# Two bf16 matrices packed into 4-byte words for the TensorE transposes of a sliding-window attention backward pass

## The chip, the cores and the metric

The kernel runs on one core of a Trainium2 chip. The core has five engines that work side by side and wait for each other through semaphores: TensorE (PE; the loading of its stationary operand is shown apart, as PEld), VectorE (DVE), ScalarE (ACT), GpSimd (POOL) and SyncE (SP), which here only issues DMAs. Matmuls write to PSUM; the other operands lie in SBUF. The metric is the device time of one execution in microseconds (us), the median of several runs.

## The reference

One forward pass and all of its gradients. The forward pass mixes a sliding-window attention branch and a gated feed-forward branch, with S = 2048 rows, D = 512, 32 heads of 16, a window of 256 and F = 1376, all in bf16:

```python
def _A_ref(x, wqkv, wo):
    H = 32; Dh = D // H; W = 256
    q, k, v = ...
    scores = einsum("bhqd,bhkd->bhqk", q, k) * (Dh ** -0.5)
    mask = (idx[:, None] - idx[None, :] >= 0) & (idx[:, None] - idx[None, :] < W)
    p = softmax(where(mask, scores, -1e9), axis=-1)
    o = einsum("bhqk,bhkd->bhqd", p, v)
    return merge_heads(o) @ wo

def _B_ref(x, W_gate, W_up, W_down):
    gate = x @ W_gate; up = x @ W_up
    gate = gate * (gate > 0)
    return (gate * up) @ W_down

g = sigmoid((x * gate_w).sum(-1))
out = g * _A_ref(x, ...) + (1 - g) * _B_ref(B_x, ...)
```

The kernel returns `out` and the gradients of x, wqkv, wo, W_gate, W_up, W_down and gate_w for a given grad_out.

## The kernel before

It has three phases, one after the other in time. The first (up to about 260 us of the span) is the feed-forward branch, forward and backward. The third (from about 790 us) computes the output and the gradient of x, row block by row block. The second, between them, is the attention branch, forward and backward in one sweep, and the change lies in it.

**Units.** The attention phase works through 360 units, listed in `units`. A unit is a group `c` of 8 heads (there are four), a block `j` of 128 queries, a block `kb` of 128 keys and a `half`: the four even or the four odd heads of the group (`HH` = 4). A query block sees three key blocks: its own (role "d", diagonal), the one before (role "m", middle) and the one before that (role "f", far). For a full query block the order is middle, far, diagonal for one half and middle, diagonal, far for the other.

**What one unit does.** `front` (L643 on) issues the scores matmul ST (L649, keys by 4 heads x 128 queries, 512 columns) and ACT's exponential of it, Pu (L655); for diagonal and far units POOL then clears the masked part (L657, L660). `front_dp` issues the matmul dPT (L669), the gradient with respect to the probabilities. `gradp` multiplies Pu by dPT on DVE into Pd (L674). `rowsum` issues eight small matmuls, for each of the four heads one with Pu as the stationary operand (L683) and one with Pd (L685), which add into BA. `flip` (L694 on) transposes Pu and Pd, so that queries lie on the partitions: for most diagonal units by one DMA transpose (L697), for the others by eight TensorE transposes (L706, four of Pu and four of Pd, each 128 x 128 with the identity `ident` as the moving operand) into one PSUM tile `pt` of 128 x 1024 bf16, which ACT and DVE copy to SBUF (`p2`) in turns, through the helper `evac` (L72 ACT, L74 DVE). `cd_piece` uses the transposed halves as stationary operands of eight small matmuls per unit (L488, L491), which add into CD, the gradients of keys and values; ACT copies CD out (L494).

**Order.** It is written out by hand in the main loop, one unit per iteration `n`. An iteration issues, in this order: `front` of unit n, `gradp` of unit n-1, the DMA transpose of unit n-2 if it has one, `rowsum` and the TensorE `flip` of unit n-3, `front_dp` of unit n, one or two `cd_piece`s from a queue, and, by a running credit, pieces of background work (the projections of the next heads and rows, L129 and L132, and weight gradients, L588 and L591). Each engine takes its instructions in that order.

**Buffers.** Middle and far units keep Pu and Pd in tiles of their own, with four buffers each; diagonal units keep both halves side by side in one tile `PP`, four buffers. The transposed tiles `p2` have six buffers for diagonal units, five for middle and four for far ones. `pt` has two PSUM buffers, CD and BA one each, and ST, dPT and the projections share four.

Of the kernel before, what the change touches and what calls it, by code (L numbers as in the profile page):

```python
# [8 lines left out]
ACT = mybir.ActivationFunctionType  # L9
ALU = mybir.AluOpType  # L10
AX = mybir.AxisListType
BF = mybir.dt.bfloat16
F32 = mybir.dt.float32
# [9 lines left out]
def kernel(  # L23
# [20 lines left out]
    nc = tc.nc  # L44
    P = 128
# [7 lines left out]
    Dh = D // H  # L53
# [13 lines left out]
    def evac(out, in_, eng=None):  # L67
        if eng is None:
            eng = ("act", "dve")[rr["i"] % 2]
            rr["i"] += 1  # L70
        if eng == "act":
            nc.scalar.copy(out, in_)  # L72
        elif eng == "dve":
            nc.vector.tensor_copy(out, in_)  # L74
        else:
            nc.gpsimd.tensor_copy(out, in_)
# [10 lines left out]

    cpool = ctx.enter_context(tc.tile_pool(name="const", bufs=1))
    ident = cpool.tile([P, P], BF, name="ident")
    gw_b = cpool.tile([P, D], BF, name="gw_b")  # L90
    g_all = cpool.tile([P, NT], F32, name="g_all")
    omg_all = cpool.tile([P, NT], F32, name="omg_all")
# [20 lines left out]
    if True:  # L113
        HH = HG // 2
# [74 lines left out]
    with ExitStack() as p1, tc.manual_schedule():  # L189
# [39 lines left out]
        nc.vector.memset(tiny[:], 0.0)  # L229
        nc.scalar.activation(tiny[:], tiny[:], ACT.Sigmoid)  # L230
        make_identity(nc, ident[:])
        wps0 = ps1.tile([P, TGW], F32, tag="mm", bufs=3, name="warm_ps")
        for _ in range(WARM):
            nc.tensor.matmul(wps0[:], lhsT=warm[:, 0:P], rhs=warm[:], start=True, stop=True)
# [76 lines left out]
        for fc in range(FC):  # L311
            for tg in range(NTG):
                k = Step()
# [90 lines left out]
        for n in range(N1 + 8):  # L404
# [22 lines left out]
            if at(6):  # L427
                f = weights(at(6))
# [30 lines left out]
    if True:  # L459
# [4 lines left out]
        wk = p3b.enter_context(tc.tile_pool(name="attw", bufs=2))  # L464
        pps = ExitStack()
        ps = pps.enter_context(tc.tile_pool(name="attps", bufs=2, space=PSUM))
# [6 lines left out]
        P2 = {}  # L473
# [6 lines left out]
        def cd_piece(c, kb, qb, half, last):  # L480
            if (c, kb) not in CDs:
                CDs[(c, kb)] = [ps.tile([P, HG, 2 * Dh], F32, tag="CD", bufs=1, name="CD"), True]
            cd = CDs[(c, kb)]
            rq = RQ[(c, qb)]
            p2 = P2[(c, qb, kb, half)]
            for hh in range(HH):
                h = 2 * hh + half
                nc.tensor.matmul(cd[0][:, h, :], lhsT=p2[:, 0, hh, :], rhs=rq[:, h, 0:2 * Dh],  # L488
                                 start=cd[1], stop=True, skip_group_check=True)
                cd[1] = False  # L490
                nc.tensor.matmul(cd[0][:, h, 0:Dh], lhsT=p2[:, 1, hh, :], rhs=rq[:, h, 2 * Dh:3 * Dh],  # L491
                                 start=False, stop=True, skip_group_check=True)
            if last:
                nc.scalar.copy(sts[c][:, kb, 1:3, :].rearrange("p a (h d) -> p h a d", h=HG),  # L494
                               cd[0][:].rearrange("p h (a d) -> p h a d", a=2))
                if kb == NT // 2 - 1 or (kb == NT - 1 and c == DC - 1):
                    spill(c, kb + 1 - NT // 2)

        def spill(c, t0):
            tsl = slice(t0, t0 + NT // 2)  # L500
            eng = nc.gpsimd if (c == DC - 1 and t0 > 0) else nc.sync
            eng.dma_start(dqkvo_d[t0 * P:(t0 + NT // 2) * P, c * 4 * P:(c + 1) * 4 * P].rearrange("(t p) n -> p t n", p=P),
                          sts[c][:, tsl, :, :].rearrange("p t a n -> p t (a n)"))
# [124 lines left out]
        for c in range(DC):  # L628
            for j in range(NT):
                kbs = [k for k in (j - 1, j, j - 2) if k >= 0]  # L630
                for half in range(2):
                    order = kbs if half or len(kbs) < 3 else [kbs[0], kbs[2], kbs[1]]
                    for ki, kb in enumerate(order):
                        u = Unit()
# [8 lines left out]
        def front(u):  # L643
            tg, jl = u.j // TPG, u.j % TPG
            z = zt[(u.c * NTG + tg) % ZB]
            KTt = proj[(u.c, u.kb // TPG)][f"K{u.half}"]
            ksl = slice((u.kb % TPG) * P, (u.kb % TPG + 1) * P)
            ST = ps.tile([P, HH, P], F32, tag="M", bufs=4, name="ST")
            nc.tensor.matmul(ST[:], lhsT=KTt[:, ksl], rhs=z[:, 0, jl, :, :], start=True, stop=True)  # L649
            if u.role == "d":  # L650
                u.PP = wk.tile([P, 2, HH, P], BF, tag="PP", bufs=4, name="PP")
                u.Pu, u.Pd = u.PP[:, 0, :, :], u.PP[:, 1, :, :]
            else:
                u.Pu = wk.tile([P, HH, P], BF, tag="Pu", bufs=4, name="Pu")
            nc.scalar.activation(u.Pu[:], ST[:], ACT.Exp)  # L655
            if u.role == "d":
                nc.gpsimd.affine_select(out=u.Pu[:], in_=u.Pu[:], compare_op=ALU.is_ge, fill=0.0, base=0,  # L657
                                        pattern=[[0, HH], [1, P]], channel_multiplier=-1)
            elif u.role == "f":
                nc.gpsimd.affine_select(out=u.Pu[:], in_=u.Pu[:], compare_op=ALU.is_ge, fill=0.0, base=-1,  # L660
                                        pattern=[[0, HH], [-1, P]], channel_multiplier=1)

        def front_dp(u):
# [5 lines left out]
            nc.tensor.matmul(u.dPT[:], lhsT=VTt[:, ksl], rhs=z[:, 1, jl, :, :], start=True, stop=True)  # L669

        def gradp(u):
            if u.role != "d":
                u.Pd = wk.tile([P, HH, P], BF, tag="Pd", bufs=4, name="Pd")
            nc.vector.tensor_tensor(out=u.Pd[:], in0=u.Pu[:], in1=u.dPT[:], op=ALU.mult)  # L674

        def rowsum(u):
            kv = proj[(u.c, u.kb // TPG)]["kv"]
# [16 lines left out]
        def flip(u):  # L694
            if u.dma:
                p2 = wk.tile([P, 2, HH, P], BF, tag="P2d", bufs=6, name="p2")
                nc.sync.dma_start_transpose(out=p2[:].rearrange("p a h q -> p (a h) q"),  # L697
                                            in_=u.PP[:].rearrange("p a h q -> p (a h q)"))
                P2[(u.c, u.j, u.kb, u.half)] = p2
                return  # L700
            eng = ("act", "dve")[copier["i"] % 2]
            copier["i"] += 1
            pt = ps.tile([P, 2, HH, P], BF, tag="TR", name="pt")
            for a, src in enumerate((u.Pu, u.Pd)):
                for hh in range(HH):
                    nc.tensor.transpose(pt[:, a, hh, :], src[:, hh, :], ident[:])  # L706
            p2 = wk.tile([P, 2, HH, P], BF, tag=f"P2{u.role}", bufs={"d": 6, "m": 5, "f": 4}[u.role], name="p2")
            evac(p2[:], pt[:], eng)
            P2[(u.c, u.j, u.kb, u.half)] = p2

        def small_ops(c, j, s):
            rows = proj[(c, j // TPG)]["rows"]
# [87 lines left out]
        with tc.manual_schedule():  # L800
# [20 lines left out]
            while n <= NU + LAG or ev or cdq or bgq:  # L821
                now = ev.pop(n, [])
                u = units[n] if n < NU else None
# [22 lines left out]
                if 1 <= n <= NU:  # L846
                    gradp(units[n - 1])
# [3 lines left out]
                if 2 <= n < NU + 2 and units[n - 2].dma:  # L851
                    flip(units[n - 2])
                if LAG <= n < NU + LAG:
                    w = units[n - LAG]
# [18 lines left out]
                for _ in range(2 if len(cdq) > 6 or (len(cdq) > 1 and cdq[1][5] and cdq[1][0] <= n and cdq[1][2] < NT - 1) else 1):  # L873
                    if cdq and cdq[0][0] <= n:
                        cd_piece(*cdq.pop(0)[1:])
                        credit -= 0.2
# [43 lines left out]
    with ExitStack() as p56:  # L920
        x_r5 = x_r

        with ExitStack() as p6:
# [5 lines left out]
            for g in range(NG):  # L929
# [3 lines left out]
                for tl in range(GT):  # L933
# [8 lines left out]
                    for c in range(DC):  # L942
# [16 lines left out]
                                            op=ALU.mult)  # L959
# [62 lines left out]
```

## Time and profile before

| | |
|---|---|
| median of three runs | 984.72 us (984.12 to 984.91) |
| the profiled execution's span | 983.5 us |
| PE busy | 949.9 us, 97%, 11528 matmuls |
| PEld busy | 612.1 us, 62% |
| DVE / ACT / POOL busy | 507.4 / 487.5 / 486.4 us |
| mean granted TensorE clock | 0.993 of full speed |
| TensorE transposes at L706 | 1888, of which 32 for diagonal units |
| BA matmuls, L683 and L685, of middle and far units | 928 and 928 |
| CD matmuls, L488 and L491, of all units | 1440 and 1440 |

A row of a group names line, engine, operation, what is written and read, the tile's shape (partitions x elements) and the count; then its busy time in us, the mean ns of one, and the idle time of the engine just ahead of it with what ended that. In matmul rows the moving operand is named first and the stationary one second, so `pt<-ident,Pd` streams the identity past a stationary Pd. Matmuls are pipelined: the record of one lasts until its last result has come out, so the rate is read from the distance between two starts and not from the length of a record. A line of the busy times by stretch gives the stretch in us, its length, then for PE, PEld, DVE, ACT and POOL the busy time and the number of instructions, and at last the granted clock, the DMA engines' share and GB/s.

### The profile page before, as it was taken

The page shows a single profiled execution, that of the slowest core. Times are in us where ns is not written, and L with a number is a line of the kernel's source. Part 1 is how long each engine was busy: PE and PEld are TensorE (multiplying, and loading weights), DVE is VectorE, ACT ScalarE, POOL GpSimd, SP SyncE. Part 2 cuts the span into 40 slices and gives each one's busy share as a digit, 9 for nine tenths or more (in the row PEclk, how much of TensorE's full clock was granted, in tenths as well). Part 3 has the DMA queues.
Part 4 walks back from the last instruction along what each step waited for, and adds up shares of the span by engine and source line. Part 5 has one row for each costly group of instructions (what it writes and reads, how often), then busy time and mean ns, then how long its engine had stood idle before and what let it go on. Part 6 is the DMA issues. An engine that isn't in the chain of part 4 may idle for free.

```text
span 983.5 us, 28082 instructions
## 1 busy us (share of the span) xinstructions
PE 949.9 (97%) x11528; PEld 612.1 (62%) x11528; DVE 507.4 (52%) x934; ACT 487.5 (50%) x825; POOL 486.4 (49%) x935
## 2 busy tenths in 40 slices
PE   8999999999999999999999999999999999999993
PEld 5555555666567777677676777766777744444441
DVE  4443322233477777666676666766666513223221
ACT  5422222222378877677686777767777611001000
POOL 1644345444176667655676566665656612221220
PEclk9999999999999999999999999999999999999997
DMA  9989999997546777765759556799969887788720
GB/s 283 195 186 214 214 214 225 213 200 172 134 82 100 98 137 134 137 119 92 132 103 175 119 86 133 109 151 155 167 108 212 178 225 195 199 202 202 175 56 16
DMA packets 415201, 153.55 MB, mean 156 GB/s; under 512 B 333568, under 2 KB 412768, under 8 KB 415072
## 3 DMA queue, kind: packets, MB, share of 16 engines
q1 hardware_dynamic: 392672, 128.67, 67.6%
q10 hardware_dynamic: 20592, 17.84, 6.3%
q0 software_dynamic: 1808, 5.24, 1.5%
q8 instruction: 90, 1.47, 0.6%
q14 instruction: 39, 0.32, 0.1%
HBM read 38.44 MB, written 38.41 MB: 78 GB/s over the span
## 4 chain that ended last, share of the span: by engine, by line
PE 83%; DMA 5%; issue 3%; POOL 3%; DVE 2%; ACT 1%; SPq 1%; ACTq 0%; POOLq 0%; DVEq 0%
PE pt L706 10%; PE ST L649 8%; PE dPT L669 7%; PE dxps L968 7%; PE wps L373 6%; PE BA L683 5%; PE pp L129 4%; PE wps L588 4%; PE dxps L985 4%; PE CD L488 4%; PE bps L939 4%; PE dhps L326 3%; PE dps L375 3%; PE ups L326 3%; PE gps L326 2%
## 5 line engine op out<-in xcount | busy, mean ns | idle before, releaser
L674 DVE TENSOR_TENSOR Pd<-Pu,dPT 128x512 bf16<-128x512 bf16 x232 | 154.5, 677 | 68.3 <-POOL Pu L660 59.1
L655 ACT ACTIVATE Pu<-ST 128x512 bf16<-128x512 f32 x232 | 139.0, 601 | 62.6 <-PE ST L649 60.1
L649 PE MATMUL ST<-z,K 128*128 128x512 bf16 x360 | 136.0, 378 | 3.9 <-DVE wst_end L74 1.2
L669 PE MATMUL dPT<-z,V 128*128 128x512 bf16 x360 | 136.1, 378 | 0.5
L72 ACT COPY p<-pt 128x1024 bf16<-128x1024 bf16 x118 | 119.6, 1014 | 12.2 <-PE pt L706 9.3
L657 POOL TENSOR_SCALAR_AFFINE_SELECT PP<-PP 128x512 bf16<-128x512 bf16 x128 | 81.2, 634 | 79.0 <-ACT PP L655 77.9
L340 POOL TENSOR_TENSOR hT<-rg,upm 128x512 bf16<-128x512 bf16 x44 | 52.3, 1189 | 124.7 <-DVE upm L338 97.1
L488 PE MATMUL CD<-rq,p 128*128 128x32 bf16 x1440 | 109.4, 177 | 1.6 <-ACT rows_st L494 1.6
L373 PE MATMUL wps<-dgu_r,x_r 128*128 128x256 bf16 x704 | 105.6, 273 | 4.8 <-DVE wst L74 4.8
L491 PEld LDWEIGHTS <-p 128*128 128x128 bf16 x1440 | 86.1, 96 | 35.5 <-issue 1.9
L491 PE MATMUL CD<-rq,p 128*128 128x16 bf16 x1440 | 106.6, 169 | 0.0
L488 PEld LDWEIGHTS <-p 128*128 128x128 bf16 x1440 | 98.8, 96 | 1.0 <-issue 0.7
L674 DVE TENSOR_TENSOR PP<-PP,dPT 128x512 bf16<-128x512 bf16 x128 | 87.3, 682 | 23.1 <-POOL PP L657 20.9
L373 PEld LDWEIGHTS <-x_r 128*128 128x128 bf16 x704 | 68.8, 98 | 36.5 <-issue 6.1
L706 PE MATMUL pt<-ident,Pd 128*128 128x128 bf16 x928 | 89.7, 219 | 0.0
L655 ACT ACTIVATE PP<-ST 128x512 bf16<-128x512 f32 x128 | 77.1, 602 | 25.0 <-PE ST L649 22.5
L706 PE MATMUL pt<-ident,Pu 128*128 128x128 bf16 x928 | 89.0, 217 | 0.0
L74 DVE COPY p<-pt 128x1024 bf16<-128x1024 bf16 x118 | 81.1, 687 | 14.3 <-PE pt L706 13.1
L660 POOL TENSOR_SCALAR_AFFINE_SELECT Pu<-Pu 128x512 bf16<-128x512 bf16 x112 | 71.0, 634 | 32.6 <-ACT Pu L655 32.0
L946 ACT COPY a_sb<-aps 128x512 f32<-128x512 f32 x16 | 9.4, 585 | 145.8 <-issue 133.1
L685 PEld LDWEIGHTS <-Pd 128*128 128x128 bf16 x928 | 57.6, 96 | 35.0 <-issue 12.2
L683 PE MATMUL BA<-KV,Pu 128*128 128x33 bf16 x928 | 76.7, 178 | 1.8 <-ACT BAs L689 1.4
(154 smaller groups left out, 1969.5 us busy)
## 6 DMA issues: line engine op xcount, KB each, us to landing
dqkvo_d<-rows_st SPq DMA_DIRECT2D x7, 1024.0 KB, 5.8
dar<-da_d SPq DMA_DIRECT2D x28, 256.0 KB, 4.6
hT_d<-hT ACTq DMA_DIRECT2D x44, 128.0 KB, 2.6
dgT_d<-dgu ACTq DMA_DIRECT2D x44, 128.0 KB, 3.0
duT_d<-dgu ACTq DMA_DIRECT2D x44, 128.0 KB, 2.9
duT_g<-duT_d SPq DMA_DIRECT2D x8, 640.0 KB, 5.3
dgT_g<-dgT_d SPq DMA_DIRECT2D x7, 640.0 KB, 5.1
gt<-hT_d SPq DMA_DIRECT2D x7, 640.0 KB, 5.6
```

The source lines that it names most:

```text
L72: nc.scalar.copy(out, in_)
L74: nc.vector.tensor_copy(out, in_)
L373: nc.tensor.matmul(acc["w"][:, c, :], lhsT=x_r[:, t, c * P:(c + 1) * P], rhs=k.dgu_r[:, :, i, :], start=(go_ and c % 2 == 0), stop=no_, sk ...
L488: nc.tensor.matmul(cd[0][:, h, :], lhsT=p2[:, 0, hh, :], rhs=rq[:, h, 0:2 * Dh], start=cd[1], stop=True, skip_group_check=True)
L491: nc.tensor.matmul(cd[0][:, h, 0:Dh], lhsT=p2[:, 1, hh, :], rhs=rq[:, h, 2 * Dh:3 * Dh], start=False, stop=True, skip_group_check=True)
L649: nc.tensor.matmul(ST[:], lhsT=KTt[:, ksl], rhs=z[:, 0, jl, :, :], start=True, stop=True)
L655: nc.scalar.activation(u.Pu[:], ST[:], ACT.Exp)
L657: nc.gpsimd.affine_select(out=u.Pu[:], in_=u.Pu[:], compare_op=ALU.is_ge, fill=0.0, base=0, pattern=[[0, HH], [1, P]], channel_multiplier=-1)
L669: nc.tensor.matmul(u.dPT[:], lhsT=VTt[:, ksl], rhs=z[:, 1, jl, :, :], start=True, stop=True)
L674: nc.vector.tensor_tensor(out=u.Pd[:], in0=u.Pu[:], in1=u.dPT[:], op=ALU.mult)
L683: nc.tensor.matmul(BA[:, h, 0:33], lhsT=u.Pu[:, hh, :], rhs=kv[:, u.kb % TPG, h, 1:34], start=(u.first and hh == 0), stop=True, skip_group ...
L706: nc.tensor.transpose(pt[:, a, hh, :], src[:, hh, :], ident[:])
```

## The change

For middle and far units, Pu and Pd no longer have tiles of their own. One tile W of 128 x 4 x 128 fp32 words is allocated in `front`. Seen as bf16, each word is a pair: Pd is the lower half of every word and Pu the upper half. The exponential, POOL's select and DVE's product write and read their half with a step of two bf16 (4 bytes), and so do the BA matmuls that take Pu and Pd as the stationary operand. `flip` transposes W as fp32, with an fp32 identity `ident_w` made at the start: four transposes of 128 x 128 words per unit in place of eight of 128 x 128 bf16. The PSUM tile has the same bytes (512 fp32 in place of 1024 bf16 per partition), and ACT and DVE copy it out as fp32 in the same turns. `cd_piece` then takes the two halves of the copied words, again with a step of two bf16. Diagonal units keep their layout and their transposes. The number of buffers for W is four.

```diff
@@ -87,6 +87,7 @@
 
     cpool = ctx.enter_context(tc.tile_pool(name="const", bufs=1))
     ident = cpool.tile([P, P], BF, name="ident")
+    ident_w = cpool.tile([P, P], F32, name="ident_w")
     gw_b = cpool.tile([P, D], BF, name="gw_b")
     g_all = cpool.tile([P, NT], F32, name="g_all")
     omg_all = cpool.tile([P, NT], F32, name="omg_all")
@@ -229,6 +230,7 @@
         nc.vector.memset(tiny[:], 0.0)
         nc.scalar.activation(tiny[:], tiny[:], ACT.Sigmoid)
         make_identity(nc, ident[:])
+        make_identity(nc, ident_w[:])
         wps0 = ps1.tile([P, TGW], F32, tag="mm", bufs=3, name="warm_ps")
         for _ in range(WARM):
             nc.tensor.matmul(wps0[:], lhsT=warm[:, 0:P], rhs=warm[:], start=True, stop=True)
@@ -485,10 +487,10 @@
             p2 = P2[(c, qb, kb, half)]
             for hh in range(HH):
                 h = 2 * hh + half
-                nc.tensor.matmul(cd[0][:, h, :], lhsT=p2[:, 0, hh, :], rhs=rq[:, h, 0:2 * Dh],
+                nc.tensor.matmul(cd[0][:, h, :], lhsT=p2[0][:, hh, :], rhs=rq[:, h, 0:2 * Dh],
                                  start=cd[1], stop=True, skip_group_check=True)
                 cd[1] = False
-                nc.tensor.matmul(cd[0][:, h, 0:Dh], lhsT=p2[:, 1, hh, :], rhs=rq[:, h, 2 * Dh:3 * Dh],
+                nc.tensor.matmul(cd[0][:, h, 0:Dh], lhsT=p2[1][:, hh, :], rhs=rq[:, h, 2 * Dh:3 * Dh],
                                  start=False, stop=True, skip_group_check=True)
             if last:
                 nc.scalar.copy(sts[c][:, kb, 1:3, :].rearrange("p a (h d) -> p h a d", h=HG),
@@ -651,13 +653,15 @@
                 u.PP = wk.tile([P, 2, HH, P], BF, tag="PP", bufs=4, name="PP")
                 u.Pu, u.Pd = u.PP[:, 0, :, :], u.PP[:, 1, :, :]
             else:
-                u.Pu = wk.tile([P, HH, P], BF, tag="Pu", bufs=4, name="Pu")
-            nc.scalar.activation(u.Pu[:], ST[:], ACT.Exp)
+                u.W = wk.tile([P, HH, P], F32, tag="W", bufs=4, name="W")
+                pair = u.W[:].bitcast(BF).rearrange("p h (q w) -> p h q w", w=2)
+                u.Pd, u.Pu = pair[:, :, :, 0], pair[:, :, :, 1]
+            nc.scalar.activation(u.Pu, ST[:], ACT.Exp)
             if u.role == "d":
-                nc.gpsimd.affine_select(out=u.Pu[:], in_=u.Pu[:], compare_op=ALU.is_ge, fill=0.0, base=0,
+                nc.gpsimd.affine_select(out=u.Pu, in_=u.Pu, compare_op=ALU.is_ge, fill=0.0, base=0,
                                         pattern=[[0, HH], [1, P]], channel_multiplier=-1)
             elif u.role == "f":
-                nc.gpsimd.affine_select(out=u.Pu[:], in_=u.Pu[:], compare_op=ALU.is_ge, fill=0.0, base=-1,
+                nc.gpsimd.affine_select(out=u.Pu, in_=u.Pu, compare_op=ALU.is_ge, fill=0.0, base=-1,
                                         pattern=[[0, HH], [-1, P]], channel_multiplier=1)
 
         def front_dp(u):
@@ -669,9 +673,7 @@
             nc.tensor.matmul(u.dPT[:], lhsT=VTt[:, ksl], rhs=z[:, 1, jl, :, :], start=True, stop=True)
 
         def gradp(u):
-            if u.role != "d":
-                u.Pd = wk.tile([P, HH, P], BF, tag="Pd", bufs=4, name="Pd")
-            nc.vector.tensor_tensor(out=u.Pd[:], in0=u.Pu[:], in1=u.dPT[:], op=ALU.mult)
+            nc.vector.tensor_tensor(out=u.Pd, in0=u.Pu, in1=u.dPT[:], op=ALU.mult)
 
         def rowsum(u):
             kv = proj[(u.c, u.kb // TPG)]["kv"]
@@ -696,17 +698,26 @@
                 p2 = wk.tile([P, 2, HH, P], BF, tag="P2d", bufs=6, name="p2")
                 nc.sync.dma_start_transpose(out=p2[:].rearrange("p a h q -> p (a h) q"),
                                             in_=u.PP[:].rearrange("p a h q -> p (a h q)"))
-                P2[(u.c, u.j, u.kb, u.half)] = p2
+                P2[(u.c, u.j, u.kb, u.half)] = (p2[:, 0, :, :], p2[:, 1, :, :])
                 return
             eng = ("act", "dve")[copier["i"] % 2]
             copier["i"] += 1
-            pt = ps.tile([P, 2, HH, P], BF, tag="TR", name="pt")
-            for a, src in enumerate((u.Pu, u.Pd)):
-                for hh in range(HH):
-                    nc.tensor.transpose(pt[:, a, hh, :], src[:, hh, :], ident[:])
-            p2 = wk.tile([P, 2, HH, P], BF, tag=f"P2{u.role}", bufs={"d": 6, "m": 5, "f": 4}[u.role], name="p2")
+            if u.role == "d":
+                pt = ps.tile([P, 2, HH, P], BF, tag="TR", name="pt")
+                for a, src in enumerate((u.Pu, u.Pd)):
+                    for hh in range(HH):
+                        nc.tensor.transpose(pt[:, a, hh, :], src[:, hh, :], ident[:])
+                p2 = wk.tile([P, 2, HH, P], BF, tag="P2d", bufs=6, name="p2")
+                evac(p2[:], pt[:], eng)
+                P2[(u.c, u.j, u.kb, u.half)] = (p2[:, 0, :, :], p2[:, 1, :, :])
+                return
+            pt = ps.tile([P, HH, P], F32, tag="TR", name="pt")
+            for hh in range(HH):
+                nc.tensor.transpose(pt[:, hh, :], u.W[:, hh, :], ident_w[:])
+            p2 = wk.tile([P, HH, P], F32, tag=f"P2{u.role}", bufs={"m": 5, "f": 4}[u.role], name="p2")
             evac(p2[:], pt[:], eng)
-            P2[(u.c, u.j, u.kb, u.half)] = p2
+            pair = p2[:].bitcast(BF).rearrange("p h (k w) -> p h k w", w=2)
+            P2[(u.c, u.j, u.kb, u.half)] = (pair[:, :, :, 1], pair[:, :, :, 0])
 
         def small_ops(c, j, s):
             rows = proj[(c, j // TPG)]["rows"]
```

## The prediction

> **What bounds the kernel now.** I read the page first, then the busy times by stretches of the span, the chain of waits inside the attention loop, the timeline of one iteration, and the groups of instructions by shape.
>
> ```profile
> PE 949.9 (97%) x11528; PEld 612.1 (62%) x11528; DVE 507.4 (52%) x934; ACT 487.5 (50%) x825; POOL 486.4 (49%) x935
> ...
> PE 83%; DMA 5%; issue 3%; POOL 3%; DVE 2%; ACT 1%; SPq 1%; ACTq 0%; POOLq 0%; DVEq 0%
> ...
> 267.00:780.00 513.00, 507.20 (x8834) 369.77 (x8833) 361.21 (x657) 381.35 (x641) 332.88 (x775) 1.00 0.73 130
> ```
>
> PE has 83% of the chain that ended last. The third line is the stretch that the change touches, the attention loop (first transpose at 267.2 us, last at 779.4): 513 us, PE busy for 507, DVE 361, ACT 381, POOL 333, granted clock 1.00. Before it lie 267 us (feed-forward) and after it 204 us (output phase), which hold none of the edited work.
>
> Busy PE time is modelled, so I go by the distance from one start to the next, which the timeline gives:
>
> ```profile
> 501.02 0.17 PE L685 MATMUL BA<-KV,Pd 128*128 128x17 bf16 x1
> 501.04 0.18 PE L683 MATMUL BA<-KV,Pu 128*128 128x33 bf16 x1
> 501.07 0.17 PE L685 MATMUL BA<-KV,Pd 128*128 128x17 bf16 x1
> 501.09 0.18 PE L683 MATMUL BA<-KV,Pu 128*128 128x33 bf16 x1
> ...
> 501.19 0.38 PE L706 MATMUL pt<-ident,Pu 128*128 128x128 bf16 x4
> 501.41 0.39 PE L706 MATMUL pt<-ident,Pd 128*128 128x128 bf16 x4
> 501.64 0.38 PE L669 MATMUL dPT<-z,V 128*128 128x512 bf16 x1
> 501.85 0.18 PE L488 MATMUL CD<-rq,p 128*128 128x32 bf16 x1
> ```
>
> Small matmuls, each with its own weight load, follow each other every 25 ns. Eight transposes take from 501.19 to 501.64, 0.45 us, 56 ns each. A matmul of 512 columns holds PE for 0.215 us (501.64 to 501.85). Taking every PE matmul of the loop at such a distance gives 497 us; the remaining 15 us are longer gaps, most of them between ST and the first BA matmul. So PE's in-order stream is the loop's clock, and a nanosecond added to or taken from that stream shows up nearly in full, until another engine's chain takes over.
>
> ```profile
> L706 PE MATMUL pt<-ident,Pd 128*128 128x128 bf16 x928 | 89.7, 219 | 0.0
> L706 PE MATMUL pt<-ident,Pu 128*128 128x128 bf16 x928 | 89.0, 217 | 0.0
> L685 PEld LDWEIGHTS <-Pd 128*128 128x128 bf16 x928 | 57.6, 96 | 35.0 <-issue 12.2
> L683 PE MATMUL BA<-KV,Pu 128*128 128x33 bf16 x928 | 76.7, 178 | 1.8 <-ACT BAs L689 1.4
> L72 ACT COPY p<-pt 128x1024 bf16<-128x1024 bf16 x118 | 119.6, 1014 | 12.2 <-PE pt L706 9.3
> L74 DVE COPY p<-pt 128x1024 bf16<-128x1024 bf16 x118 | 81.1, 687 | 14.3 <-PE pt L706 13.1
> ```
>
> 928 + 928 transposes over 8 make 232 changed units (the other 32 at this line belong to four diagonal units, which stay). They hold PE for 232 x 0.45 = 104.4 us.
>
> **The change, part by part.**
>
> *Transposes.* 1856 of 128 bf16 columns become 928 whose data and identity are fp32. No row has a 4-byte operand on PE, so the price is bounded. From below: a column costs the same whatever its width, 56 ns, and the unit goes from 0.45 to 0.224 us, -52.4 us over 232 units. From above: a word is two 16-bit halves in the data and two in the identity, so four products of 128 columns, which is a 512-column row, 0.215 us, 0.86 us per unit, 199.5 us in all, **+95.1 us**. Break-even is 112 ns. I take the upper end: all rows from 128 to 512 columns cost strictly by column of 2-byte numbers, and nothing in the trace shows the array taking more than 2 bytes per operand in a step; a transpose that has to return all 32 bits unchanged can drop none of the products.
>
> The Trainium skill, "FP8 and Floating Point Precision", TensorE Precision Notes, says that true fp32 takes four passes through the array; by it the sum would be 928 x 4 x 56 = 208 us, +103.5 us. No run so far shows an fp32 matmul here.
>
> *Weight loads.* Pu and Pd, and their transposed halves, are now every second bf16 of a row. They are the weights of 8 BA and 8 CD matmuls per unit, 16 x 232 = 3712 loads. From below they cost nothing more: 25 ns is also the distance of 17-column and 33-column matmuls alike, so something other than the operand sets it. From above, the overlap is lost and the whole 96 ns of a load's record shows: 71 ns x 3712 = +264 us. I take 0, being nearest to the same instruction with the same 128 columns, and keep the upper end as a rival.
>
> *Exp, select and product* write and read at a 4-byte step: 232 exp (601 ns), 112 selects (634 ns), 232 products (677 ns). The products already have a 4-byte operand, dPT in PSUM. Even 100 ns more on each puts ACT at 381 + 23 and DVE at 361 + 23 of 513 us, so other iterations' PE work hides it: 0. Were PE no longer the cover, the chain exp, select, product would be 0.3 us longer per far unit, 112 x 0.3 = 34 us at most.
>
> *Copies out of PSUM.* ACT's 118 copies go from 1024 bf16 (1014 ns) to 512 fp32; the nearest row, a_sb of 512 fp32 from PSUM, takes 585 ns, so ACT loses 118 x 0.43 = 51 us of work. DVE's go from 687 to about the 692 ns of its 512-element fp32 casts. Neither is on the path: no PE wait in the loop names these copies. Worth 0, at best a part of the 15 us of gaps.
>
> *Buffers and the rest.* W holds Pu and Pd from the exp on, four buffers as each had before. Units run middle, far, diagonal, middle, diagonal, far, so the fifth changed unit is six iterations after the first, whose transposes come three iterations after its exp: no new wait. The second identity adds a memset and a select on POOL (0.20 and 0.29 us for the first) ahead of a 12.4 us idle stretch; with no such cover it would be 0.5 us. No DMA is added or moved, on any queue.
>
> *The gaps.* Slower transposes give the exp, select, product chain 0.41 us more per unit, which covers part of the 15 us; I take half, -8 us (bounds 0 and -15).
>
> Sum against the profiled execution: span 983.5 + 95.1 - 8 = 1070.6 us. The median of the runs is 984.7, 1.2 us more than that span, so **1072 us**. This case's own range, with the gaps from 0 to -15 and the transpose at 54 to 56 ns a pass, is 1064 to 1090.
>
> **Rivals.**
>
> *One pass, priced by bytes.* 128 words are as many bytes as 256 columns of bf16, and the 256-column rows of the feed-forward phase are 108 ns apart. The unit then takes 0.434 us: -0.016 x 232 = -3.7 us, **981 us**, with 0 to -15 for gaps that the lighter ACT closes and some tens of nanoseconds per unit the other way, 966 to 992. For it: all PE rows scale with bytes as well as with columns. Against: it needs the array to carry 32 bits through in one go.
>
> *One pass at the column rate* (the other side). PE reads a word as easily as a half and returns it whole: 56 ns, -52.4 us, 932 us; the iteration gets shorter, and up to 15 us comes back as waits of PE for the exp, select, product chain, which already make the gaps. **940 us**, 932 to 950. It decides from a transpose under 112 ns. For it: cost by column is the only rule that the rows state. Against: all of them are bf16.
>
> The Trainium skill, "TensorE: Matmul & The Clock Gate", Terms, lists a transpose mode that is 4x faster for fp32; by that rule this rival holds. No row here shows it.
>
> *The load is exposed.* If the weight load of a 4-byte tile isn't overlapped with the transpose before it, each costs 96 + 56 = 152 ns, 0.61 us a unit, +0.16 x 232 = 37 us, **1021 us**. Against: every load in the rows above is hidden.
>
> The same page of the skill, Weight-path perf modes, leaves fp32 out of its fast weight load.
>
> *Strided weights.* If half of each word read is thrown away and a pair goes from 25 to 50 ns, 3712 x 25 = +93 us on top of any of these; with the one pass by bytes **1074 us**, with the forecast 1165. Its limit is the +264 us above. Against: the 25 ns doesn't look like the load's own time.
>
> **How the numbers follow.** Forecast 0.38; one pass by bytes 0.25; one pass by column 0.12; exposed load 0.12; strided weights 0.13. A measurement of this kernel (984.1 to 984.9) can tell about 0.2%, 2 us. The one-pass-by-bytes case straddles zero: of its 0.25 I give 0.14 to faster, 0.06 to same, 0.05 to slower. Faster is 0.12 + 0.14 = 0.26, same 0.06, slower 0.38 + 0.12 + 0.13 + 0.05 = 0.68. The range takes in all but the upper part of the strided case: from 932 (the column rate without any loss) to 1100.
>
> **What would show it.** In the changed profile, the line of the fp32 transposes: their number (928 if a word goes through in one instruction, more if it is split), and the distance from the first transpose of a unit to the dPT matmul after it: 0.86 us by the forecast, 0.43, 0.22 and 0.61 by the rivals. BA and CD pairs must stay 25 ns apart; if they are wider, strided weights are at work. ACT's copies should be near 585 ns, and the stretch before 267 us unchanged. A transpose under 112 ns with 25 ns pairs makes the prediction wrong.

## The result and the profile after

The changed kernel takes 992.88 us (median of four runs, 992.63 to 994.99) beside 984.42 us for the kernel before (four runs): a ratio of 1.0090, 95% interval 1.0076 to 1.0104. The profiled execution's span is 991.3 us, against 983.5 before. The change is slower, as forecast, but by 8.5 us and not by 87.

The page of the changed kernel, its busy times, its chain and the groups that answer to those of before (line, engine, operation, shapes and count; then busy us and mean ns of one; then idle time before):

```profile
PE 955.6 (96%) x10600; PEld 615.1 (62%) x10600; DVE 515.3 (52%) x934; ACT 479.5 (48%) x825; POOL 499.2 (50%) x937
...
PE 76%; POOL 9%; DVE 4%; issue 4%; DMA 4%; ACT 1%; SPq 1%; ACTq 0%; POOLq 0%; DVEq 0%
...
L659 ACT ACTIVATE W<-ST 128x512 bf16<-128x512 f32 x232 | 175.6, 758 | 80.8 <-PE ST L651 74.2
L676 DVE TENSOR_TENSOR W<-W,dPT 128x512 bf16<-128x512 bf16 x232 | 166.7, 734 | 79.9 <-POOL W L664 72.7
L716 PE MATMUL pt<-ident_w,W 128*128 128x128 f32 x928 | 147.4, 281 | 0.0
...
L664 POOL TENSOR_SCALAR_AFFINE_SELECT W<-W 128x512 bf16<-128x512 bf16 x112 | 85.8, 766 | 33.3 <-ACT W L659 31.6
...
L716 PEld LDWEIGHTS pt<-ident_w,W 128*128 128x128 f32 x928 | 97.2, 141 | 0.0
L659 ACT ACTIVATE PP<-ST 128x512 bf16<-128x512 f32 x128 | 76.8, 600 | 31.6 <-PE ST L651 27.4
```

The same three operations of the kernel before:

```profile
L674 DVE TENSOR_TENSOR Pd<-Pu,dPT 128x512 bf16<-128x512 bf16 x232 | 154.5, 677 | 68.3 <-POOL Pu L660 59.1 <-PE dPT L669 6.9 <-PE ST L649 1.3
L655 ACT ACTIVATE Pu<-ST 128x512 bf16<-128x512 f32 x232 | 139.0, 601 | 62.6 <-PE ST L649 60.1
...
L660 POOL TENSOR_SCALAR_AFFINE_SELECT Pu<-Pu 128x512 bf16<-128x512 bf16 x112 | 71.0, 634 | 32.6 <-ACT Pu L655 32.0
```

Three things are to be seen. There are 928 fp32 transposes, one instruction per four-byte tile, so nothing was split into passes that show. The strided exp (758 ns against 601 before, and 600 for the diagonal units, which still write at unit step), select (766 against 634 before) and product (734 against 677) are all longer; exp and select by more than the 100 ns that I allowed for. And POOL and DVE have 13% of the chain that ended last, where they had 5%.

The timeline of one unit of the changed kernel:

```profile
502.28 0.18 PE L685 MATMUL BA<-KV,W 128*128 128x33 bf16 x1
502.31 0.17 PE L687 MATMUL BA<-KV,W 128*128 128x17 bf16 x1
502.33 0.63 PE L716 MATMUL pt<-ident_w,W 128*128 128x128 f32 x4
502.81 0.38 PE L673 MATMUL dPT<-z,V 128*128 128x512 bf16 x1
```

BA pairs are still 25 ns apart, although their weights are strided. The four transposes hold PE from 502.33 to 502.81. From the single starts in the trace, the first takes 144 ns until the next starts and the other three 109 ns each: 471 ns a unit, where eight bf16 transposes took 444. (The start of the first is the usual 25 ns behind the last BA matmul; the extra 35 ns lie between its start and that of the second.)

For all runs I use one ledger, worked out from the starts of the PE matmuls: the loop is the time from the first ST to the last CD; the transposes are the usual time per unit times the number of units (with 1.8 us for the four diagonal ones); all other matmuls at their usual distance are 408.7 us in every kernel; what remains are gaps. Each row is one profiled execution. What lies outside the loop stayed between 450.0 and 453.5 us in all executions of this table and of the one further down, and the loop's difference to the kernel before agrees with that of the medians to within 2.8 us, so a difference of gaps below 2 or 3 us says little by itself. In four traces (marked *) some of the 512-column records are missing, so the gaps there are this remainder, and what is counted from single gaps is approximate.

| kernel | loop, us | transposes, us (ns a unit) | gaps, us | ratio to before (95%) |
|---|---|---|---|---|
| before | 530.9 | 104.7 (444) | 17.5 | 1 |
| changed | 539.1 | 111.1 (471) | 19.3 | 1.0090 (1.0076 to 1.0104) |
| layout alone* | 536.3 | 104.7 (444) | 22.9 | 1.0058 (1.0042 to 1.0075) |
| fp32 transposes alone* | 535.4 | 111.1 (471) | 15.6 | 1.0056 (1.0040 to 1.0071) |
| changed, word exp | 535.7 | 111.1 (471) | 15.9 | 1.0058 (1.0038 to 1.0077) |
| changed, dPT first* | 534.9 | 102.6 (434) | 23.6 | 1.0049 (1.0033 to 1.0065) |
| before, dPT first* | 533.2 | 104.9 (444) | 19.6 | 1.0046 (1.0028 to 1.0064) |
| changed, transposes first | 534.6 | 102.9 (436) | 23.0 | 1.0040 (1.0026 to 1.0054) |
| before, transposes first | 527.2 | 105.0 (445) | 13.4 | 0.9960 (0.9946 to 0.9974) |
| before, copies as words | 531.1 | 104.7 (444) | 17.6 | 1.0008 (0.9996 to 1.0020) |

Between the two kernels the loop grew by 8.2 us: 6.4 in the transposes and 1.8 in the gaps. The 1.8 is small beside the spread, but the waits counted below grow by as much.

### The profile page after: what moved, and what is told of

It is laid out like the page before. It is cut to its first block, busy times and chain, and to the rows that moved or that the text cites. A ratio compares the mean times of both kernels' runs of the same rounds, so it can differ in the third digit from the quotient of the medians.

```text
span 991.3 us, 26230 instructions
## 1 busy us (share of the span) xinstructions
PE 955.6 (96%) x10600; PEld 615.1 (62%) x10600; DVE 515.3 (52%) x934; ACT 479.5 (48%) x825; POOL 499.2 (50%) x937
## 4 chain that ended last, share of the span: by engine, by line
PE 76%; POOL 9%; DVE 4%; issue 4%; DMA 4%; ACT 1%; SPq 1%; ACTq 0%; POOLq 0%; DVEq 0%
PE pt L716 8%; PE dxps L979 7%; PE wps L375 6%; PE ST L651 6%; PE dPT L673 6%; PE pp L130 4%; PE wps L590 4%; PE dxps L996 4%; PE bps L950 4%; PE BA L685 3%; PE CD L490 3%; PE dhps L328 3%; PE dps L377 3%; PE ups L328 3%; PE gps L328 3%
## 5 line engine op out<-in xcount | busy, mean ns | idle before, releaser
L659 ACT ACTIVATE W<-ST 128x512 bf16<-128x512 f32 x232 | 175.6, 758 | 80.8 <-PE ST L651 74.2
L676 DVE TENSOR_TENSOR W<-W,dPT 128x512 bf16<-128x512 bf16 x232 | 166.7, 734 | 79.9 <-POOL W L664 72.7
L716 PE MATMUL pt<-ident_w,W 128*128 128x128 f32 x928 | 147.4, 281 | 0.0
L664 POOL TENSOR_SCALAR_AFFINE_SELECT W<-W 128x512 bf16<-128x512 bf16 x112 | 85.8, 766 | 33.3 <-ACT W L659 31.6
L716 PEld LDWEIGHTS pt<-ident_w,W 128*128 128x128 f32 x928 | 97.2, 141 | 0.0
L74 DVE COPY p<-pt 128x512 f32<-128x512 f32 x118 | 80.7, 684 | 10.8 <-PE pt L716 10.6
L687 PEld LDWEIGHTS <-W 128*128 128x128 bf16 x928 | 57.9, 97 | 33.6 <-issue 10.9
L685 PEld LDWEIGHTS <-W 128*128 128x128 bf16 x928 | 68.3, 97 | 15.9 <-issue 2.5
L685 PE MATMUL BA<-KV,W 128*128 128x33 bf16 x928 | 76.7, 178 | 1.5 <-ACT BAs L691 1.5
```

The lines of the kernel that those rows point to most:

```text
L659: nc.scalar.activation(u.Pu, ST[:], ACT.Exp)
L664: nc.gpsimd.affine_select(out=u.Pu, in_=u.Pu, compare_op=ALU.is_ge, fill=0.0, base=-1, pattern=[[0, HH], [-1, P]], channel_multiplier=1)
L676: nc.vector.tensor_tensor(out=u.Pd, in0=u.Pu, in1=u.dPT[:], op=ALU.mult)
L685: nc.tensor.matmul(BA[:, h, 0:33], lhsT=u.Pu[:, hh, :], rhs=kv[:, u.kb % TPG, h, 1:34], start=(u.first and hh == 0), stop=True, skip_group ...
L716: nc.tensor.transpose(pt[:, hh, :], u.W[:, hh, :], ident_w[:])
```

## Experiments

**The two halves of the change, each alone.** My theory after the result: PE's own time for the transposes makes the whole loss. Rival: the slower exp, select and product make it.

```diff
-            pt = ps.tile([P, HH, P], F32, tag="TR", name="pt")
-            for hh in range(HH):
-                nc.tensor.transpose(pt[:, hh, :], u.W[:, hh, :], ident_w[:])
...
+            pt = ps.tile([P, 2, HH, P], BF, tag="TR", name="pt")
+            for a, src in enumerate((u.Pu, u.Pd)):
+                for hh in range(HH):
+                    nc.tensor.transpose(pt[:, a, hh, :], src[:, hh, :], ident[:])
...
```

> The interleaved tile W alone: exp, select and product write and read every second bf16, BA takes its weights from them, but each unit is transposed as before by eight bf16 transposes (from strided weights), copied out as 1024 bf16, and CD's weights are contiguous. Theory (the loss is PE's: the four fp32 transposes of a unit take 479 ns where eight bf16 ones took 444): the loss is gone, 984 to 986 us, ratio to before 1.000 to 1.002, a unit's transposes again 444 ns, although exp stays near 758 ns, select near 766 and product near 734. Rival (the slower exp, select and product delay PE): about as slow as the changed kernel, 991 to 995 us, with the loss in PE's gaps. Third (strided weights slow the transposes): transposes over 56 ns apart.

Measured: 988.82 us beside 982.69. The transposes are at 444 ns again, 55 to 56 ns each from strided weights, so the third idea is out. But the loss isn't gone: 5.4 us of new gaps. My theory was wrong in saying that the layout costs nothing, and the rival was wrong in making it everything.

```diff
-                pair = u.W[:].bitcast(BF).rearrange("p h (q w) -> p h q w", w=2)
-                u.Pd, u.Pu = pair[:, :, :, 0], pair[:, :, :, 1]
+                pair = u.W[:].bitcast(BF).rearrange("p (a x) q -> p a (x q)", a=2).rearrange(...)
+                u.Pu, u.Pd = pair[:, 0, :, :], pair[:, 1, :, :]
```

> The fp32 transposes alone: Pu and Pd lie contiguous in W, so exp, select and product work at unit step, and a 4-byte word is two neighbouring queries of one matrix; four fp32 transposes, fp32 copies, strided CD weights as in the changed kernel. The rows that come out are paired differently, so the gradients of keys and values are not those of the reference. Theory: the whole loss is here, 991 to 994 us, 479 ns per unit, exp back at 601 ns, select 634, product 677. Rival (strided producers): near 984 to 986 us.

Measured: 988.50 us, ratio 1.0056: two thirds of the loss, not all of it. Exp is at 599 ns, select at 634, product at 677, a unit's transposes at 471 ns as in the changed kernel, and the gaps at 15.6 us, a little less than before. My reading is that slower PE work gives the other engines more room (the lighter copies alone, tested below, left the gaps at 17.6). Together the parts cost 8.5 us, alone 6.1 and 5.8, which fits: where PE is slower, part of the strided operations' extra time is hidden.

Where the gaps of the layout come from is seen in the waits of PE. Of the kernel before, of the layout alone and of the changed kernel with the transposes first (what waits, for whom, us in all, times, longest):

```profile
PE ST L649 <- DVE PP L674: 1.2, 2, 0.8
PE ST L649 <- DVE Pd L674: 0.8, 2, 0.5
```

```profile
PE ST L651 <- DVE W L676: 3.5, 13, 0.7
...
PE ST L651 <- DVE PP L676: 1.0, 2, 0.6
```

```profile
PE ST L651 <- DVE W L676: 5.0, 15, 0.9
```

ST waits for DVE's product of an earlier unit, which reads dPT in one of the four PSUM tiles that ST, dPT and the projections share. The chain behind that product is, for a far unit, exp, select, product: 601 + 634 + 677 ns before, 758 + 766 + 734 with the step. The view has four such waits before and 15 with the layout, 2.0 and 4.5 us, less than the 5.4 us of new gaps, because it counts only what is left when the record of the matmul ahead has ended. Counted from the single starts, the gaps of PE that end 50 to 56 ns after the end of a product are 5.5 us in 20 places before, about 10.7 in 46 with the layout alone, 7.2 in 28 in the changed kernel and about 4.0 in 13 with the fp32 transposes alone. So they make up nearly all of the layout's 5.4 us and of the changed kernel's 1.8.

**Which part of the step slows exp and select.** Exp writes full words, and DVE then overwrites the lower half.

```diff
-            nc.scalar.activation(u.Pu, ST[:], ACT.Exp)
+            nc.scalar.activation(u.Pu if u.role == "d" else u.W[:], ST[:], ACT.Exp)
-                nc.gpsimd.affine_select(out=u.Pu, in_=u.Pu, ... base=-1,
+                nc.gpsimd.affine_select(out=u.W[:], in_=u.W[:], ... base=-1,
```

> The changed kernel, but exp writes whole fp32 words at unit step and the far units' select works on whole words; DVE's product then overwrites the lower half of each word. Pu is the truncated upper half of the fp32 exponential and no longer a rounded bf16. Theory (what slows exp and select is the 2-byte write at a 4-byte step): exp back near 601 ns, select near 634, product still near 734; of the 2 to 5 us of PE gaps that the strided layout costs, 1 to 4 go: 988 to 991 us where the changed kernel is 991 to 993 beside the same runs of before, transposes unchanged at 471 ns a unit. Rival (the 4-byte step of the following reads and of the product is what costs): no change, ratio as the changed kernel, 1.009. Rival (4-byte elements are slow for exp and select as such): exp over 700 ns, select over 700.

The groups of this kernel:

```profile
L676 DVE TENSOR_TENSOR W<-W,dPT 128x512 bf16<-128x512 bf16 x232 | 166.3, 733 | 68.5 <-POOL W L664 53.7 <-PE dPT L673 12.0 <-PE CD L493 1.9
...
L659 ACT ACTIVATE W<-ST 128x512 f32<-128x512 f32 x232 | 139.1, 599 | 86.6 <-PE ST L651 82.0
...
L664 POOL TENSOR_SCALAR_AFFINE_SELECT W<-W 128x512 f32<-128x512 f32 x112 | 71.1, 635 | 32.1 <-ACT W L659 30.1 <-DMA z<-zT 2.0
```

Exp and select at unit step take 599 and 635 ns, though they write twice the bytes. So the size of the element costs nothing here, and 2-byte elements at a 4-byte step cost 159 and 131 ns per 512. The product stays at 733 ns. Gaps fall from 19.3 to 15.9 us, the waits for a product from 7.2 to 4.1 and the ratio to 1.0058: the layout's part in the changed kernel is about 3.4 us, nearly all of it through exp and select. Which of these two counts more isn't separated.

**The 144 ns.** The load of the unit's first transpose starts 23 ns before the transpose, and 35 ns are too many; by these two numbers I estimate a 4-byte load of weights at 58 ns. A long matmul ahead would hide it.

```diff
                     rowsum(w)
+                    if u is not None:
+                        front_dp(u)
                     if not w.dma:
                         flip(w)
...
-                if u is not None:
+                if u is not None and n < LAG:
                     front_dp(u)
```

> The changed kernel with the dPT matmul issued between the BA matmuls and the transposes rather than behind them. Theory (a 4-byte weight load takes about 58 ns, is hidden behind the 109 ns of an fp32 transpose, but only 23 ns of the unit's first load are hidden behind a 25 ns BA matmul): the first transpose of a unit drops from 144 to 109 ns, a unit to 436 ns, 8 us less than the changed kernel, 983 to 986 us. Rival (the extra 35 ns is the switch from bf16 to fp32 on PE, not the load): first transpose still 144 ns, 991 to 994 us. Rival (load bound): all four gaps change.

> The kernel before with the same move of dPT ahead of the transposes: what the order alone does. Theory: bf16 loads are hidden behind 25 ns already, so the transposes stay at 444 ns; dPT comes 0.44 us earlier, which can only shorten the product's wait; 980 to 985 us. If the order alone is worth several us, the gain of the run before this one is not the load's.

Measured: the first transpose falls to 108 ns, a unit to 434, as the theory has it, 8.5 us less PE work than in the changed kernel. The switch from bf16 to fp32 is still there, so a switch that costs 35 ns whatever stands ahead is out; a switch that a long matmul can hide would look like the load, and no run separates the two. The time is 987.54 us, ratio 1.0049, and not 983 to 986: the gaps rose to 23.6 us. The control shows that this order also costs the kernel before: 987.13 us, ratio 1.0046, where I expected 980 to 985.

```diff
-                    rowsum(w)
                     if not w.dma:
                         flip(w)
+                    rowsum(w)
```

> The changed kernel with the four transposes issued between ST and the BA matmuls rather than behind BA; dPT keeps its place. Theory (the first fp32 load needs about 58 ns of cover): behind the 215 ns of ST it is hidden, a unit's transposes take 436 instead of 471 ns, 8 us of PE work less than in the changed kernel, and as dPT isn't moved no new gaps: ratio to before 1.000 to 1.004. Rival (any move of the transposes costs several us of gaps, as the move of dPT did): ratio 1.004 to 1.009 although the first transpose is at 109 ns.

> The kernel before with the eight bf16 transposes issued between ST and BA: what that order alone does. Theory (order costs gaps, apart from any fp32 load): transposes 444 ns as before, gaps of the loop up from 17.5 to about 20 to 24 us, ratio 1.002 to 1.006. Rival (the order costs nothing for bf16): ratio 0.999 to 1.001, and the gaps of the changed kernel in this order come from its strided producers.

With ST ahead the first transpose is again at 109 ns. One unit of the changed kernel in this order, 0.43 us:

```profile
504.69 0.38 PE L651 MATMUL ST<-z,K 128*128 128x512 bf16 x1
504.91 0.60 PE L716 MATMUL pt<-ident_w,W 128*128 128x128 f32 x4
505.34 0.18 PE L685 MATMUL BA<-KV,W 128*128 128x33 bf16 x1
```

Its ratio, 1.0040, lies where the ranges of theory and rival meet; its gaps, 23.0 us, are the rival's, as I had expected no new ones. The control went against me: bf16 transposes between ST and BA make the kernel before faster, 979.56 us, ratio 0.9960, with the gaps down to 13.4 us. So in this order the changed kernel loses 0.8% to its control although its transposes are 9 ns a unit cheaper; all of that is gaps, 23.0 against 13.4 us. The loss of the change isn't tied to the exposed load: take that away, and the layout's share grows. Why this order suits bf16 is seen in the gaps between ST and BA: 8.4 us before, 1.3 us with the transposes in between. In the kernel before, 41 of these gaps, 8.2 us, end 51 to 53 ns after the end of ACT's copy of BA, as here:

```profile
500.44 0.50 ACT L689 COPY BAs<-BA 128x400 f32<-128x400 f32 x1
...
500.58 0.38 PE L649 MATMUL ST<-z,K 128*128 128x512 bf16 x1
...
500.99 0.18 PE L683 MATMUL BA<-KV,Pu 128*128 128x33 bf16 x1
```

BA has one PSUM tile, so the first BA matmul of a query block waits until ACT has copied the sums of the one before. With the transposes ahead of BA three such gaps, 1.0 us, are left. The changed kernel gains nearly as much by it (7.1 to 1.0 us), but there the waits for a product rise from 7.2 to 12.2 us, and in the kernel before only from 5.5 to 8.5.

**The lighter copies alone.**

```diff
-            evac(p2[:], pt[:], eng)
...
+                evac(p2[:].rearrange(...).bitcast(F32), pt[:].rearrange(...).bitcast(F32), eng)
```

> The kernel before, eight bf16 transposes and contiguous Pu and Pd, but the copy out of PSUM moves 512 fp32 words in place of 1024 bf16 for middle and far units: the change's lighter copies alone. Theory: ACT's copy falls from 1014 to about 585 ns, DVE's stays at 687, PE's work is as before; worth 0 to 3 us of PE's gaps, ratio 0.997 to 1.000. Rival (ACT's queue is what holds up exp and so PE): 10 us or more, ratio under 0.990.

Measured: 984.02 us beside 983.47, ratio 1.0008 (0.9996 to 1.0020). ACT's copy takes 588 ns in place of 1014, and nothing comes of it: the copies were not on the path.

**What the 109 ns are.** One run, measured once, with the transposes split into halves of 64 keys:

```diff
-                nc.tensor.transpose(pt[:, hh, :], u.W[:, hh, :], ident_w[:])
+                for x in range(2):
+                    r = slice(64 * x, 64 * x + 64)
+                    nc.tensor.transpose(pts[x][:, hh, :], u.W[r, hh, :], ident_w[r, r])
...
```

> The changed kernel, each 128 x 128 fp32 transpose split into two of 64 keys (stationary 64 partitions x 128 queries, a 64 x 64 identity streamed past) into two PSUM banks, copied out by ACT and DVE, one half each; one unit's transposes then wait for the copies of the unit before. Theory (109 ns is the time in which 128 fp32 columns stream past): a half takes about 55 ns, a pair 109 if the halves go one after the other, 55 to 60 if both halves of the array work at once. Rival (109 ns is the weight load's time, 128 columns either way): 109 ns per half, a unit at 0.87 us. The whole time is expected to be longer than the changed kernel's because of the waits for the copies, 1000 to 1060 us.

Measured: 1014.29 us, with 60 us of gaps, as expected for its waits. The halves do work side by side: by the single starts in its trace the two halves of a pair start 4 ns apart, and the pairs are 62 ns apart. So 109 ns is not the time of a weight load of 128 columns, which is in each half too. The first pair takes 112 ns, and from the last one to the next full-size matmul it is 155 ns, so these two cost about 50 and 97 ns more than a pair in the middle. There is a third cost, which the ledger puts among the gaps: the first half starts 101 ns after the last BA matmul (100 to 108 in all units) in place of 25. Over 232 units these 76 ns are nearly 18 of the 60 us.

**A version that beats both.** Two units per entry, with and without words, and once more between ST and BA:

> The changed kernel with exp writing whole words, the fp32 transposes split into two halves of 64 keys in two PSUM banks, and two units (middle and far, or two middle) transposed in one go, so that the entry (108 ns) and the exit (155 ns) that the run of the split transposes showed are paid once per two units; four half copies per two units. Theory (the halves work side by side, 60 to 62 ns a pair): 8 pairs in about 0.64 us, 0.32 us a unit against 0.444 before and 0.471 changed, 28 us less PE work than before, 15 to 25 us of gaps: ratio to before 0.968 to 0.985. Rival (coarser work on PE makes gaps that eat it): loop gaps over 40 us, ratio over 0.99.

> The run of the paired halves with the transposes between ST and BA. Theory (the entry is an uncovered fp32 load): the first pair drops from 108 to about 62 ns, 23 ns a unit, 5 us; with the gaps that an order like this cost in the changed kernel (about 4 us more), within 5 us of the other order. Rival (the entry is a switch of the array's mode): first pair still 108 ns.

> The kernel before (bf16, contiguous Pu and Pd, no words) with the transposes of two units at a time split into halves of 64 keys in two PSUM banks, copied out as fp32 words: whether side-by-side halves need the 4-byte words at all. Theory (each small matmul still takes its turn of 25 ns): 32 halves at 25 ns, about 0.9 us per two units, 0.45 a unit, no gain, ratio 0.998 to 1.010. Rival (a pair of halves goes in about 30 ns): 0.31 us a unit, a gain like that of the words, ratio 0.965 to 0.985, without the strided producers.

The core of the last, on the kernel before (PSUM tiles of 128 x 2 x 2 x 4 x 64 bf16, one bank for each half):

```diff
+            waiting.append(u)
+            if len(waiting) < 2:
+                return
...
+            for i, v in enumerate(two):
+                for a, src in enumerate((v.Pu, v.Pd)):
+                    for hh in range(HH):
+                        for x in range(2):
+                            r = slice(64 * x, 64 * x + 64)
+                            nc.tensor.transpose(pts[x][:, i, a, hh, :], src[r, hh, :], ident[r, r])
```

| kernel | loop, us | transposes, us (ns a unit) | gaps, us | time, us | ratio to before (95%) |
|---|---|---|---|---|---|
| paired halves, words, word exp | 525.1 | 76.5 (322) | 39.9 | 980.25 | 0.9963 (0.9950 to 0.9976) |
| the same between ST and BA | 541.4 | 76.5 (322) | 56.2 | 995.15 | 1.0124 (1.0108 to 1.0140) |
| paired halves, bf16 | 519.3 | 68.3 (287) | 42.3 | 973.02 | 0.9890 (0.9876 to 0.9904) |

The first of them I had expected with 15 to 25 us of gaps and a ratio of at most 0.985; its gaps, 39.9 us, take back most of the gain, much as the rival had it. The second, expected within 5 us of the first, is 15 us slower: 22.1 us of its gaps, in 44 places, end 50 to 52 ns after the end of ACT's copy of BA, against 1.9 us in four places in the first.

The timeline of the bf16 version (32 half transposes of two units, then dPT) and its chain by engine:

```profile
508.53 0.17 PE L685 MATMUL BA<-KV,Pd 128*128 128x17 bf16 x1
508.64 0.29 PE L724 MATMUL pt<-ident,Pu 64*128 64x64 bf16 x8
508.76 0.28 PE L724 MATMUL pt<-ident,Pd 64*128 64x64 bf16 x8
508.88 0.28 PE L724 MATMUL pt<-ident,Pu 64*128 64x64 bf16 x8
509.00 0.28 PE L724 MATMUL pt<-ident,Pd 64*128 64x64 bf16 x8
509.21 0.39 PE L669 MATMUL dPT<-z,V 128*128 128x512 bf16 x1
```

```profile
PE 70%; POOL 10%; DVE 9%; issue 5%; DMA 3%; ACT 2%; SPq 0%; POOLq 0%; ACTq 0%; DVEq 0%
```

My theory that each small matmul would take its turn of 25 ns fell: eight halves take 0.12 us, a pair 29 to 30 ns. The rival had that right, but its ratio, 0.965 to 0.985, was not reached. Bf16 halves are cheaper than halves of words (287 against 322 ns a unit) and need no interleaved layout. PE's transposes lost 36 us against the kernel before, of which the gaps took back 25; PE is down to 70% of the chain. Of these gaps about 9 us are the entries: the first half starts 103 ns after the last BA matmul (508.53 to 508.64), at all 116 entries within 2 ns, so it is not a wait for another engine. The waits for a product have grown from 5.5 to about 16 us. In the version with the transposes between ST and BA the first pair still took 112 ns behind the 215 ns of ST, and it started 307 ns after ST in place of 215. A load that only lacked cover would have been hidden there, as in the unsplit run (109 ns). So I read the entry as a change of the array's mode across which an fp32 load is not taken ahead; that it costs time is measured, what the array does in it is not. In bf16 the first pair takes 38 ns, 9 more than the others.

## Why the prediction was right and wrong

*What bounds the kernel* was right: PE's in-order stream is the loop's clock. 8.2 us more loop made 7.8 us more span, and 6.4 of the 8.2 are PE's own instructions.

*Transposes*: this is the step that failed. I took the upper bound, four products, 0.86 us a unit and +95.1 us, because no row showed more than two bytes per operand going through the array in a step. The run shows 109 ns per transpose of words, which is the price by bytes (108 to 109 ns for 256 columns of bf16 in the kernel before), in one instruction. The rival "one pass, priced by bytes" had the price right; its -3.7 us came from 0.45 us a unit before, where the single starts give 444 ns, so four times 109 is -8 ns a unit, -1.9 us. It lacked the 35 ns of the unit's first transpose, 8.1 us in all, which turn the -1.9 into +6.3, the 6.4 of the ledger. An exposed load was another rival, as a cost of all four transposes; only the first pays it. The break-even was put right, 112 ns, and the mean is 118. Between bounds that were 52 below and 95 us above zero, two prices, by column and by bytes, had rows behind them, which as all rows were bf16 could not tell them apart; four products had none, and I let a thought about arithmetic decide.

The Trainium skill, "FP8 and Floating Point Precision", TensorE Precision Notes, counts four passes for true fp32. The trace disagrees for a transpose: 109 ns, not 4 x 56 = 224. The Trainium skill, "TensorE: Matmul & The Clock Gate", Terms, lists a transpose mode that is four times faster for fp32, which against those four passes would be 56 ns. The measured 109 is faster by a factor of two, and no run shows whether that mode is on. The Trainium skill, same page, Weight-path perf modes, leaves fp32 out of the fast weight load. The trace fits that: the record of an fp32 load is 141 ns long against 97 in bf16, beside the 35 ns at the first transpose.

*Weight loads* at 0: right. BA and CD pairs stay 25 ns apart, and bf16 transposes from strided weights 55 to 56 ns.

*Exp, select and product* at 0: wrong twice. They rose by 157, 132 and 57 ns, the first two above the 100 that I allowed as an extreme, and the cover that I named, other iterations' PE work, was thinner than the busy sums made it look: ACT at 366 and DVE at 362 of 513 us are far from full, but ST waits for a product at the end of a chain of three. That cost 5.4 us alone and about 3.4 us beside the slower transposes.

*Copies* at 0: right, shown by the run with the lighter copies alone, 1.0008.

*The gaps* at -8 us: the sign was wrong. I had read them as waits for the exp, select, product chain, which slower transposes would cover; but 8.2 of the 17.5 us before are waits for ACT's copy of BA, and 7.1 of them are still there in the changed kernel. Slower transposes gave a little room (15.6 us with the fp32 transposes alone, -1.9), and the longer chain took more than that (19.3 in the changed kernel).

*Buffers, second identity, DMAs*: nothing of them shows in a wait of PE.

The direction was luck: the four products that were to make the kernel slower are not there, and what made it slower, the first transpose of each unit and the longer chain, had no term in the sum or stood there at 0. That the time lies in the range says little, as the range ran from 932 to 1100; at 1072 us a change of 8.5 us was foreseen as one of 87.

## What to carry to other kernels

Packing two 2-byte matrices into words didn't make PE's transposes cheaper, as a transpose of words took twice as long as one of bf16, and it made each engine that fills one half of a word slower; what it does save, a lighter copy out of PSUM, can be had by a bitcast alone, and is worth something only where the copy is on the path. Two half-height transposes into different PSUM banks work side by side, and a batch of them pays for the change to halves and back once. When a sum's bounds lie on both sides of zero, don't take a price that no row supports over one that a row does. Before a gap is counted as cover for some chain, see in the single starts what it waits for. And look for the first and the last instruction of a group, which don't cost what the middle ones do.

## What the runs showed of the hardware

- An fp32 transpose of 128 x 128 holds PE for 109 ns, a bf16 one for 55 to 56. The first one behind a 25 ns matmul holds it for 144; behind another fp32 transpose or a 512-column matmul it is 108 to 109. The 35 ns are read as the weight load.
- A write of 512 2-byte elements at a 4-byte step takes ACT 758 ns against 600 at unit step, and POOL, which also reads at the step, 766 against 634; full 4-byte words at unit step cost 599 and 635.
- Transposes of 64 partitions in the two halves of the array start 3 to 4 ns apart and run together: 29 ns a pair in bf16, 62 ns in fp32. Going over to them costs 76 to 92 ns ahead of the first half and 9 (bf16) or 50 ns (fp32) in the first pair, the return to full-size matmuls about 97 ns.
- A PE matmul that waits until ACT or DVE has read a PSUM tile starts 51 to 55 ns after the end of that instruction, in the kernel before.

The Trainium skill, "TensorE: Matmul & The Clock Gate", Part 3, says that matmuls on distinct row groups run at the same time with starts about 4 ns apart; the trace agrees, for transposes too (3 to 4 ns).
